# First bias by pieces, `past` ahead of the branch, and the first pair's q and k in units on two DMA queues

## The chip, the cores and the metric

The kernel runs on one core of one Trainium2 chip. A core has five engines that run side by side: TensorE (PE in the profile, with PEld for its weight loads), VectorE (DVE), ScalarE (ACT), GpSimd (POOL) and SyncE (SP), which in this kernel issues nearly all DMAs. Each engine takes its instructions in order; waits between engines are waits on semaphores. The metric is the device time of one execution in microseconds (us); lower is better.

## The reference, cut to what matters

One sample passes through three blocks: an attention with a band, a mask and an ALiBi bias, and two token and channel mixers. Only the start of the attention is touched here.

```python
B, H, S, D = 2, 8, 768, 64              # n_global = 8, n_local = 96
scores = scale * q @ k.T
rel = pos[:, None] - pos[None, :]
is_global = pos[None, :] < n_global
is_local = (rel >= 0) & (rel < n_local)
dist = where(is_global & ~is_local, n_local, abs(rel))
scores = where(is_global | is_local, scores - slopes[h] * dist, -1e9)
a = softmax(scores) ; attn = a @ v
x = attn as [B, S, H*D] ; x = moe(x) ; out = moe2(x)
```

## The kernel before

Attention runs in 24 **units**: two batches, four pairs of heads, and three units of two blocks of 128 queries in each pair. A unit u needs, for each of the pair's two heads, four score matmuls (L437) against the block's own 128 keys and the PREV = 96 keys before it with NG = 32 global ones, so 256 columns (128 for the first block of a sequence). VectorE adds the bias and takes the row's minimum of the negated score (L450), ScalarE takes the exponential (L574, L578), TensorE turns the result (L484), ScalarE or VectorE copies it out of PSUM (L496, L494), and TensorE multiplies with the values (L406). The loop of `attention_band` works on three units at once: scores of u, turning of u-1, values of u-2. Matmuls are recorded as several passes.

**Order.** Everything around the change is in a hand-written order (`manual_schedule`): each engine runs what is recorded for it, in the order of the code. Before the branch stand the loads of the first pair (`load_first`: two DMAs for k and two for q, of 2 and 4 blocks, all on SP), ten warming matmuls on zeros (L330), `constants`, `ramps` (three iotas on GpSimd, cast to float on ScalarE) and the first pair's values. Then every engine loads two words of `nv` into its registers (L913, first a pointer, then the value) and branches on them (L918): the band path for small n_global and n_local, a dense path otherwise.

**The bias.** Behind the branch `band_bias` makes one tile `base` of 128 x 384: `base0` (128 columns, for the first block of a sequence) and `base1` (256 columns: 96 `before`, 32 `seen`, 128 `own`). VectorE turns the counts to float (`nvf`, L290), makes `own` from `past` (a causal mask by affine select on GpSimd, L286), `before`, and the first NG columns of `base0` as the larger of `own` and `seen`; GpSimd makes `seen` (L292, L295); ScalarE copies the other 96 columns of `base0` (L308). Then each of the eight heads gets a scaled copy of all 384 columns: heads 0 and 1 on ScalarE (L317), heads 2 to 7 on GpSimd (L319).

**The loads of the next pairs.** Before the loop SP issues q and k of pair 1. In the loop, at the second unit of each pair, GpSimd sets ones in the next pair's value tiles (`tiles_v`, L360), and SP issues, in this order, that pair's v and twice a (`load_v`, L367, L369, L370), for pair 1 also a weight block (L125), and q and k of the pair after it (`load_qk`, L338, L339). In GpSimd's order the first of these `tiles_v` stands behind its six scaled copies of the bias; SP's v waits for it, and everything that SP issues later waits behind v. Numbering pairs 0 to 7, pair 1 begins with unit 3 and pair 2 with unit 6.

Of the kernel before, what the change touches and what calls it, by code (L numbers as in the profile page):

```python
# [15 lines left out]
F32 = mybir.dt.float32  # L16
# [3 lines left out]
AF = mybir.ActivationFunctionType  # L20
ALU = mybir.AluOpType
# [3 lines left out]
B, H, S, D = 2, 8, 768, 64  # L25
P = 128
NS = S // P
# [8 lines left out]
NG = 32  # L36
# [4 lines left out]
SCALE = 0.125  # L41
BIG = 2.56e11
# [14 lines left out]
def slope(h):  # L57
    return 2.0 ** (-(h + 1.0))
# [25 lines left out]
class Build:  # L84
# [139 lines left out]

    def constants(self, pool):
        nc = self.nc
        self.halfpi = pool.tile([P, 1], F32, name="halfpi")
        nc.vector.memset(self.halfpi, math.pi / 2)
        one = pool.tile([P, 1], F32, name="one")
        nc.scalar.activation(out=one, in_=self.halfpi, func=AF.Exp)  # L230
        self.ident = pool.tile([P, P], F32, name="ident")
        make_identity(nc, self.ident)

    def load_counts(self, pool):
        self.nvi = pool.tile([P, 4], I32, name="nvi")
        self.nvf = pool.tile([P, 4], F32, name="nvf")
        self.nc.sync.dma_start(out=self.nvi, in_=self.dram["nv"].broadcast_to([P, 4]))
# [24 lines left out]
    def ramps(self, pool):  # L262

        self.ramp = []
        for n, base, mult in ((P, 0, -1), (PREV, -PREV, -1), (NG, 0, 0)):
            ti = pool.tile([P, n], I32, name="ramp_i%d" % n)
            self.nc.gpsimd.iota(ti, pattern=[[1, n]], base=base, channel_multiplier=mult)
            tf = pool.tile([P, n], F32, name="ramp%d" % n)
            self.nc.scalar.copy(out=tf, in_=ti)
            self.ramp.append(tf)  # L270

    def band_bias(self, pool):

        nc = self.nc
        ng, nl = self.nvf[:, 0:1], self.nvf[:, 2:3]
        base = pool.tile([P, 3 * P], F32, name="base")  # L280
        base0, base1 = base[:, 0:P], base[:, P : 3 * P]
        before, seen, own = base1[:, 0:PREV], base1[:, PREV:P], base1[:, P : 2 * P]
        with self.tc.tile_pool(name="bb", bufs=1) as tp:
            d_own, d_prev, gcol = self.ramp
            past = tp.tile([P, P], F32, name="past")
            nc.gpsimd.affine_select(  # L286
                out=past, in_=d_own, pattern=[[-1, P]], compare_op=ALU.is_ge, fill=-BIG,
                base=0, channel_multiplier=1,
            )
            nc.vector.tensor_copy(out=self.nvf, in_=self.nvi)  # L290
            g = tp.tile([P, NG], F32, name="far_g")
            nc.gpsimd.tensor_scalar(  # L292
                out=g, in0=gcol, scalar1=ng, scalar2=-BIG, op0=ALU.is_ge, op1=ALU.mult
            )
            nc.gpsimd.tensor_scalar(out=seen, in0=g, scalar1=nl, scalar2=None, op0=ALU.subtract)  # L295
            nnl = tp.tile([P, 1], F32, name="nnl")
            nc.vector.tensor_scalar(out=nnl, in0=nl, scalar1=-1.0, scalar2=None, op0=ALU.mult)

            def near(out, t, dist, tag):

                far = tp.tile([P, t.shape[1]], F32, name="far" + tag)
                nc.vector.tensor_scalar(
                    out=far, in0=dist, scalar1=nnl, scalar2=-BIG, op0=ALU.is_le, op1=ALU.mult
                )
                nc.vector.tensor_tensor(out=out, in0=far, in1=t, op=ALU.add)

            near(own, past, d_own, "own")
            nc.scalar.copy(out=base0[:, NG:P], in_=own[:, NG:P])  # L308
            near(before, d_prev, d_prev, "prev")
            nc.vector.tensor_tensor(  # L310
                out=base0[:, 0:NG], in0=own[:, 0:NG], in1=seen, op=ALU.max
            )
        self.base = []
        for h in range(H):
            t = pool.tile([P, 3 * P], F32, name="base%d" % h)
            if h < 2:
                nc.scalar.activation(out=t, in_=base, func=AF.Copy, scale=slope(h) / SCALE)  # L317
            else:
                nc.gpsimd.tensor_scalar(  # L319
                    out=t, in0=base, scalar1=slope(h) / SCALE, scalar2=None, op0=ALU.mult  # L320
                )
            self.base.append((t[:, 0:P], t[:, P : 3 * P]))

# [16 lines left out]
    def load_first(self, pool):  # L342

        t = dict(
            q=pool.tile([P, S], F32, name="q_0_0", tag="q"),
            k=pool.tile([P, NS, KW], F32, name="k_0_0", tag="k"),
        )
        q, k = self.dram["q"][0, 0], self.dram["k"][0, 0]
        for i0, i1 in ((0, 2), (2, NS)):
            qs = slice(i0 * P, i1 * P)  # L350
            self.nc.sync.dma_start(out=t["k"][:, i0:i1], in_=k[:, i0:i1])
            self.nc.sync.dma_start(out=t["q"][:, qs], in_=q[:, qs])
        return t

# [512 lines left out]
    def run(self):  # L867
        nc, tc, dram = self.nc, self.tc, self.dram
        with ExitStack() as es:
            cp = es.enter_context(tc.tile_pool(name="const", bufs=1))  # L870
# [31 lines left out]
            with tc.tile_pool(name="pair0", bufs=1, side="right") as p0:  # L902
                with tc.manual_schedule():
                    self.load_counts(cp)
                    first = self.load_first(p0)
                    self.zero = self.x[1][:, 0, 0 : E // 2].bitcast(mybir.dt.bfloat16)
                    nc.vector.memset(self.zero, 0.0)
                    self.warm_up(WARM)
                    self.constants(cp)
                    self.ramps(p0)  # L910
                    self.tiles_v(p0, first, 0, 0)
                    self.load_v(first, 0, 0)
                    _, nv = nc.values_load_multi_w_load_instructions(dram["nv"])  # L913
                band = (
                    (nv[0] >= 0) * (nv[0] <= NG) * (nv[1] == 0)
                    * (nv[2] >= 1) * (nv[2] <= PREV + 1) * (nv[3] == 0)
                )
                with tc.If(band) as c:  # L918
                    with tc.tile_pool(name="bias", bufs=1, side="right") as bp, \
                            tc.tile_pool(name="pairs", bufs=2, side="right") as pp, \  # L920
                            tc.manual_schedule():
                        self.band_bias(bp)
                        self.attention_band(pp, first, h1)
                with c.Else():
                    self.counts(cp)
                    with tc.tile_pool(name="pairs", bufs=2, side="right") as pp:
                        self.attention_dense(pp, first, h1)
# [445 lines left out]
```

## Time and profile before

| | us |
|---|---|
| median of 3 runs (lowest, highest) | 492.79 (492.22, 492.97) |
| the profiled execution | 493.28 |
| its span in the trace | 491.5 |
| PE busy | 484.3 |
| DVE, ACT, POOL busy | 317.4, 262.9, 180.8 |

The granted TensorE clock is 1.00 over the whole span. In the trace all times count from the start of the span. A row of the timeline or of the chain gives start and duration; a row of waits gives the engine and line that waited, what ended the wait, the sum, the number and the longest; a row of a window gives, for each engine, busy time and number of instructions, then the granted clock, the busy share of the core's 16 DMA engines, and GB/s.

### The profile page before, as it was taken

What the parts mean: (1) busy time and instruction counts of PE and PEld (TensorE: products, weight loads), DVE (VectorE), ACT (ScalarE), POOL (GpSimd) and SP (SyncE); (2) the same over time, 40 slices, a digit from 0 to 9 for tenths busy, and PEclk for the clock granted to TensorE, in tenths of its full rate; (3) what the DMA queues carried; (4) which work ended last, traced back from release to release, by engine and by line L of the source; (5) the groups of instructions that cost most, each with busy time, mean ns of one, the idle gap of its engine ahead of it and who ended that gap; (6) DMA issues with size and microseconds to landing.
All of it is one profiled execution on the core that took longest, in us unless ns stands there. A gap on an engine that the chain in (4) does not pass through costs nothing.

```text
span 491.5 us, 7645 instructions
## 1 busy us (share of the span) xinstructions
PE 484.3 (99%) x2836; PEld 412.3 (84%) x2836; DVE 317.4 (65%) x671; ACT 262.9 (53%) x482; POOL 180.8 (37%) x187
## 2 busy tenths in 40 slices
PE   8999999999999999999999999999999999999997
PEld 4788888787888888888888888888888889988896
DVE  4688787854776689506656564687998866351442
ACT  6888777723565554204569464646776566322010
POOL 7345534430443575401323241334554633333000
PEclk9999999999999999999999999999999999999999
DMA  6687863401454545302444222524210101000012
GB/s 194 202 261 219 280 209 119 129 2 50 134 172 107 158 137 143 94 1 85 147 133 149 87 56 60 141 87 104 68 23 22 44 22 23 21 23 22 23 71 101
DMA packets 49022, 50.66 MB, mean 103 GB/s; under 512 B 20944, under 2 KB 39888, under 8 KB 48976
## 3 DMA queue, kind: packets, MB, share of 16 engines
q1 hardware_dynamic: 48976, 50.08, 34.6%
q8 instruction: 25, 0.41, 0.3%
q14 instruction: 21, 0.17, 0.1%
HBM read 42.21 MB, written 3.15 MB: 92 GB/s over the span
## 4 chain that ended last, share of the span: by engine, by line
PE 83%; DVE 5%; ACT 5%; POOL 3%; DMA 2%; issue 1%; DVEq 0%; SPq 0%; POOLq 0%; ACTq 0%
PE gp L96 20%; PE h L96 18%; PE y L96 13%; PE v L96 7%; PE mm L96 7%; PE o L406 5%; PE th L96 5%; PE t L484 4%; PE s L437 4%; DMA k<-k 2%; POOL base L319 1%; ACT cut_xt L789 1%; DVE x L1061 1%; DVE w L1154 1%; POOL s L1180 1%
## 5 line engine op out<-in xcount | busy, mean ns | idle before, releaser
L149 POOL TENSOR_TENSOR cvt<-cvt,cvs 128x512 int32<-128x512 int32 (+1 forms) x57 | 75.1, 1318 | 177.2 <-DVE cvt L148 144.0
L96 PE MATMUL h<-wc,g 128*128 128x512 f32 x432 | 101.7, 389 | 0.0
L96 PE MATMUL gp<-xh,wc 128*128 128x512 f32 (+1 forms) x384 | 97.1, 335 | 0.0
L96 PEld LDWEIGHTS h<-wc,g 128*128 128x128 f32 x432 | 79.6, 188 | 15.2
L96 PEld LDWEIGHTS gp<-xh,wc 128*128 128x128 f32 x384 | 67.2, 189 | 8.6 <-DVE g L708 0.2
L708 DVE SCALAR_TENSOR_TENSOR g<-gp,g 128x512 fp32r<-128x512 f32 (+1 forms) x48 | 26.7, 556 | 63.4 <-ACT g L706 63.1
L96 PE MATMUL gp<-xl,wc 128*128 128x512 f32 (+1 forms) x192 | 64.3, 335 | 0.0
L96 PE MATMUL y<-wri,s 128*128 128x256 f32 (+1 forms) x288 | 52.0, 335 | 0.2 <-POOL s L1180 0.2
L96 PE MATMUL y<-wri,z 128*128 128x256 f32 (+1 forms) x288 | 51.9, 335 | 0.0
L706 ACT ACTIVATE g<-gp 128x512 fp32r<-128x512 f32 (+1 forms) x48 | 23.4, 486 | 53.2 <-PE gp L96 53.2
L96 PEld LDWEIGHTS y<-wri,s 128*128 128x128 f32 x288 | 44.7, 189 | 6.4 <-POOL s L1180 0.4
L96 PEld LDWEIGHTS y<-wri,z 128*128 128x128 f32 x288 | 44.6, 188 | 5.9
L484 PE MATMUL t<-ident,e 128*128 128x128 f32 x176 | 48.1, 285 | 0.4 <-ACT at L496 0.4
L145 DVE SCALAR_TENSOR_TENSOR cvs<-cvt,cvs 128x512 int32<-128x512 int32 (+1 forms) x57 | 44.8, 787 | 0.1
L96 PEld LDWEIGHTS gp<-xl,wc 128*128 128x128 f32 x192 | 36.0, 188 | 4.7
L450 DVE CUSTOM_DVE_ANT_0 e<-s,base 128x256 f32<-128x256 f32 (+1 forms) x96 | 32.9, 397 | 9.1 <-PE s L437 7.1
L484 PEld LDWEIGHTS t<-ident,e 128*128 128x128 f32 x176 | 31.7, 184 | 8.1 <-issue 2.3
L139 ACT ACTIVATE cvt<-raw 128x512 f32<-128x512 f32 (+1 forms) x57 | 37.2, 653 | 2.2 <-issue 2.2
L140 ACT ACTIVATE cvs<-raw 128x512 int32<-128x512 uint16 (+1 forms) x57 | 37.4, 656 | 0.0
L96 PE MATMUL th<-s,xt 128*128 128x512 f32 x144 | 34.9, 391 | 0.0
L1157 ACT ACTIVATE w<-w 128x512 f32<-128x512 f32 x12 | 7.6, 632 | 49.4 <-DVE w L1154 49.4
L406 PE MATMUL o<-v,at 128*128 128x65 f32 x192 | 32.3, 252 | 0.0
(111 smaller groups left out, 839.9 us busy)
## 6 DMA issues: line engine op xcount, KB each, us to landing
raw<-w_ch SPq DMA_DIRECT2D x28, 512.0 KB, 4.1
raw<-w_tok SPq DMA_DIRECT2D x21, 512.0 KB, 4.2
k<-k SPq DMA_DIRECT2D x7, 480.0 KB, 5.6
v<-v SPq DMA_DIRECT2D x8, 384.0 KB, 3.7
out<-o SPq DMA_DIRECT2D x11, 256.0 KB, 2.0
q<-q SPq DMA_DIRECT2D x7, 384.0 KB, 4.7
raw<-w_theta SPq DMA_DIRECT2D x4, 512.0 KB, 4.0
a<-v SPq DMA_DIRECT2D x8, 240.0 KB, 4.5
```

Of the source, the lines that this page charges most:

```text
L96: self.nc.tensor.matmul(out, lhsT=a, rhs=b, start=first and i == 0, stop=last and i == n - 1)
L139: nc.scalar.activation(out=f(t), in_=f(top), func=AF.Copy, scale=2.0**-111)
L140: nc.scalar.activation(out=s, in_=nxt, func=AF.Copy, scale=2.0**-13)
L145: nc.vector.scalar_tensor_tensor(out=s, in0=t, scalar=-(1 << 31), in1=s, op0=ALU.bitwise_and, op1=ALU.bitwise_or)
L149: nc.gpsimd.tensor_tensor(out=t, in0=t, in1=s, op=ALU.add)
L406: self.nc.tensor.matmul(po[:, j * OW : j * OW + D + 1], lhsT=at, rhs=v[:, j * (D + 1) : (j + 1) * (D + 1)], start=first, stop=last,)
L437: nc.tensor.matmul(ps[j][:, ii, c0:], lhsT=t["q"][pj, i * P : (i + 1) * P], rhs=kf[pj, i * KW - P + c0 : i * KW + P], start=True, stop=True,)
L450: nc.vector.tensor_tensor_reduce(out=e, in0=ps[j][:, ii, c0:], in1=self.base[2 * hp + j][min(i, 1)], op0=ALU.add, op1=ALU.min, scale=-SCAL ...
L484: nc.tensor.transpose(pt[:, ii, c, :], e[j][:, ii, c * P : (c + 1) * P], self.ident)
L706: nc.scalar.activation(out=hi, in_=ps, func=AF.Relu if relu else AF.Copy)
L708: nc.vector.scalar_tensor_tensor(out=lo, in0=ps, scalar=0.0, in1=f(hi), op0=ALU.max, op1=ALU.subtract)
L1157: nc.scalar.activation(out=a, in_=t, func=AF.Abs)
```

## The change

- `constants` is split: a new `table`, called first, sets `halfpi` and starts ScalarE's table load; only `ident` stays in `constants`.
- `load_first` loads q and k in three pieces of two blocks each. q stays on SP. The first piece of k stays on SP, the other two are issued from ScalarE's queue, behind its table.
- `ramps` casts the iotas on VectorE and no longer on ScalarE, and makes `past` there, ahead of the branch, in a part of `x[1]` that is still free.
- In `band_bias` the larger-of of `own` and `seen` comes before `before`. Heads 0 and 1 get their bias in three pieces each: 96 columns from `own`, 32 from `base0`, 256 from `base1`. ScalarE's copy of 96 columns into `base0` stands behind these six. Heads 2 to 7 are as before on GpSimd, which reads all of `base`.

```diff
@@ constants @@
+    def table(self, pool):
+        self.halfpi = pool.tile([P, 1], F32, name="halfpi")
+        self.nc.vector.memset(self.halfpi, math.pi / 2)
+        one = pool.tile([P, 1], F32, name="one")
+        self.nc.scalar.activation(out=one, in_=self.halfpi, func=AF.Exp)
...
@@ ramps @@
-            self.nc.scalar.copy(out=tf, in_=ti)
+            self.nc.vector.tensor_copy(out=tf, in_=ti)
             self.ramp.append(tf)
+        self.past = self.x[1][:, 1, 0:P]
+        self.nc.gpsimd.affine_select(
+            out=self.past, in_=self.ramp[0], pattern=[[-1, P]], compare_op=ALU.is_ge, fill=-BIG,
+            base=0, channel_multiplier=1,
+        )
@@ band_bias @@
-            near(own, past, d_own, "own")
-            nc.scalar.copy(out=base0[:, NG:P], in_=own[:, NG:P])
-            near(before, d_prev, d_prev, "prev")
+            near(own, self.past, d_own, "own")
             nc.vector.tensor_tensor(
                 out=base0[:, 0:NG], in0=own[:, 0:NG], in1=seen, op=ALU.max
             )
...
+            near(before, d_prev, d_prev, "prev")
...
+        for h in range(2):
+            scaled(h, own[:, NG:P], NG, P)
+            scaled(h, base0[:, 0:NG], 0, NG)
+        for h in range(2):
+            scaled(h, base1, P, 3 * P)
+        nc.scalar.copy(out=base0[:, NG:P], in_=own[:, NG:P])
+        for h in range(2, H):
+            nc.gpsimd.tensor_scalar(
+                out=ts[h], in0=base, scalar1=slope(h) / SCALE, scalar2=None, op0=ALU.mult
+            )
...
@@ load_first @@
-        for i0, i1 in ((0, 2), (2, NS)):
-            qs = slice(i0 * P, i1 * P)
-            self.nc.sync.dma_start(out=t["k"][:, i0:i1], in_=k[:, i0:i1])
+        for i0 in range(0, NS, 2):
+            qs = slice(i0 * P, (i0 + 2) * P)
+            queue = self.nc.scalar if i0 else self.nc.sync
+            queue.dma_start(out=t["k"][:, i0 : i0 + 2], in_=k[:, i0 : i0 + 2])
             self.nc.sync.dma_start(out=t["q"][:, qs], in_=q[:, qs])
```

**VectorE ahead of the branch**, before (`x_66` is the tile of zeros for the warming matmuls, `ISA` begins the branch):

```order
L907 MEMSET x_66 128x256
L228 MEMSET halfpi 128x1
L913 TENSOR_LOAD nv_ptr
L913 TENSOR_LOAD nv
L918 ISA
```

and now:

```order
L232 MEMSET halfpi 128x1
L918 MEMSET x_66 128x256
L271 CAST ramp_132<-ramp_i_130 128x128 [waits Pool_49]
L271 CAST ramp_136<-ramp_i_134 128x96 [waits Pool_49]
L271 CAST ramp_140<-ramp_i_138 128x32 [waits Pool_49]
L924 TENSOR_LOAD nv_ptr
L924 TENSOR_LOAD nv
L929 ISA
```

Three casts that wait for GpSimd's iotas now stand ahead of VectorE's register loads.

**ScalarE behind the branch**, before (`base_303` and `base_305` are the bias of heads 0 and 1):

```order
L918 COMPARE_AND_BRANCH
L308 COPY base<-base 128x96 [waits DVE_49]
L317 ACTIVATE base_303<-base 128x384 [waits DVE_49,Activation_49]
L317 ACTIVATE base_305<-base 128x384
L574 ACTIVATE e_0_330<-e_0_330,mn_329 128x128 [waits DVE_49]
```

and now (heads 0 and 1 are `base_303` and `base_304`):

```order
L929 COMPARE_AND_BRANCH
L317 ACTIVATE base_303<-base 128x96 [waits DVE_49]
L317 ACTIVATE base_303<-base 128x32 [waits DVE_49]
L317 ACTIVATE base_304<-base 128x96
L317 ACTIVATE base_304<-base 128x32
L317 ACTIVATE base_303<-base 128x256 [waits DVE_49,Pool_49]
L317 ACTIVATE base_304<-base 128x256
L326 COPY base<-base 128x96
L584 ACTIVATE e_0_335<-e_0_335,mn_334 128x128 [waits DVE_49]
```

Two scaled copies became six, and the copy of 96 columns moved from ahead of them to behind them.

**GpSimd behind the branch**, before (`base_307` is head 2's bias):

```order
L918 COMPARE_AND_BRANCH
L286 AFFINE_SELECT past<-ramp_130 128x128 [waits Activation_49]
L292 TENSOR_SCALAR far_g<-ramp_138,nvf 128x32 [waits DVE_49,Activation_49]
L295 TENSOR_SCALAR base<-far_g,nvf 128x32 [waits Pool_49]
L319 TENSOR_SCALAR base_307<-base 128x384 [waits DVE_49,Activation_49]
```

and now (head 2 is `base_305`, head 3 `base_306`):

```order
L929 COMPARE_AND_BRANCH
L294 TENSOR_SCALAR far_g<-ramp_140,nvf 128x32 [waits DVE_49]
L297 TENSOR_SCALAR base<-far_g,nvf 128x32 [waits Pool_49]
L328 TENSOR_SCALAR base_305<-base 128x384 [waits DVE_49,Activation_49,Pool_49]
L328 TENSOR_SCALAR base_306<-base 128x384
```

`past` moved ahead of the branch. The first of the six scaled copies waits for VectorE and for ScalarE, as before; the ScalarE instruction that it waits for is the copy of 96 columns.

## Rows read from the trace of the kernel before

**Rows 1.** The page's part 1, TensorE: busy us, share of span, instructions.
```profile
PE 484.3 (99%) x2836; PEld 412.3 (84%) x2836; DVE 317.4 (65%) x671; ACT 262.9 (53%) x482; POOL 180.8 (37%) x187
```

**Rows 2.** Waits of PE, whole span: us in total, times, longest.
```profile
PE s L437 <- DMA q<-q: 0.8, 1, 0.8
PE s L437 <- DMA k<-k: 0.7, 1, 0.7
PE mm L96 <- ACT xh L706: 0.5, 1, 0.5
```

**Rows 3.** The chain that ended last, 0 to 25 us: start, us, what.
```profile
5.99 4.59 POOL base L319 x4
...
15.81 7.91 DMA k<-k
```

**Rows 4.** Timeline, 4 to 25 us, TensorE, GpSimd and SP's queue.
```profile
5.99 7.08 POOL L319 TENSOR_SCALAR base<-base 128x384 f32<-128x384 f32 x6 [0.39 <-DVE base L310]
13.27 0.38 SPq L367 DMA_DIRECT2D v<-v  x1
15.81 1.55 SPq L339 DMA_DIRECT2D k<-k  x1
23.86 0.93 PE L437 MATMUL s<-k,q 64*128 64x128 f32 x8 [0.70 <-DMA k<-k]
```

**Rows 5.** Line 913, the register loads by engine: ns min/median/max, first and last start.
```profile
L913 DVEq TENSOR_LOAD <-nv_ptr x1: 911/911/911, 0.8 to 0.8; - x1
L913 DVEq TENSOR_LOAD <-nv x1: 1346/1346/1346, 1.8 to 1.8; - x1
L913 ACTq TENSOR_LOAD <-nv_ptr x1: 1017/1017/1017, 2.0 to 2.0; - x1
L913 ACTq TENSOR_LOAD <-nv x1: 1051/1051/1051, 3.1 to 3.1; - x1
L913 SPq TENSOR_LOAD <-nv_ptr x1: 2880/2880/2880, 4.7 to 4.7; - x1
```

**Rows 6.** Timeline, 0 to 8 us: iotas, second k, and the bias.
```profile
1.26 0.50 POOL L267 IOTA ramp_i<- 128x128 int32 x3
2.12 0.43 SPq L351 DMA_DIRECT2D k<-k  x1
4.03 0.17 DVE L290 CAST nvf<-nvi 128x4 f32<-128x4 int32 x1 [2.89 <-DMA nvi<-nv]
4.56 0.50 POOL L292 TENSOR_SCALAR far_g<-ramp,nvf 128x32 f32<-128x32 f32 x1
5.15 0.45 POOL L295 TENSOR_SCALAR base<-far_g,nvf 128x32 f32<-128x32 f32 x1
5.28 0.27 ACT L308 COPY base<-base 128x96 f32<-128x96 f32 x1 [2.56 <-DVE base L305]
5.39 0.26 DVE L305 TENSOR_TENSOR base<-farprev,ramp 128x96 f32<-128x96 f32 x1
5.63 0.19 DVE L310 TENSOR_TENSOR base<-base 128x32 f32<-128x32 f32 x1
5.92 0.94 ACT L317 ACTIVATE base<-base 128x384 f32<-128x384 f32 x2 [0.37 <-DVE base L310]
```

**Rows 7.** Windows from v's issue to k's landing: busy, clock, DMA share, GB/s.
```profile
13.00:14.30 1.30, 1.16 (x12) 0.73 (x11) 0.71 (x3) 1.30 (x4) 0.63 (x4) 1.00 0.00 0
14.30:15.00 0.70, 0.70 (x9) 0.70 (x9) 0.66 (x5) 0.34 (x3) 0.65 (x1) 1.00 0.32 94
22.00:23.00 1.00, 1.00 (x12) 0.92 (x10) 1.00 (x5) 1.00 (x4) 0.26 (x3) 1.00 0.06 26
```

**Rows 8.** DMA queues, 15.7 to 15.8 and 16.9 to 17.0 us: packets, MB, share.
```profile
q8 instruction: 1, 0.02, 76.1%
...
q14 instruction: 1, 0.01, 35.9%
```

More of the change, by code (lines that the diff above doesn't have):

```diff
@@ L226, in constants @@
         nc = self.nc
[L227 to L230, printed above, removed]
         self.ident = pool.tile([P, P], F32, name="ident")
         make_identity(nc, self.ident)
+    def table(self, pool):
[3 more added lines that the diff above has]
+        self.nc.scalar.activation(out=one, in_=self.halfpi, func=AF.Exp)
     def load_counts(self, pool):
@@ L284, in band_bias @@
             d_own, d_prev, gcol = self.ramp
[L285 to L289, printed above, removed]
             nc.vector.tensor_copy(out=self.nvf, in_=self.nvi)
@@ L312, in band_bias, with scaled @@
             )
[L313 to L322, printed above, removed]
+            near(before, d_prev, d_prev, "prev")
+        ts = [pool.tile([P, 3 * P], F32, name="base%d" % h) for h in range(H)]
+        def scaled(h, src, c0, c1):
+            nc.scalar.activation(
+                out=ts[h][:, c0:c1], in_=src, func=AF.Copy, scale=slope(h) / SCALE
+            )
[8 more added lines that the diff above has]
+                out=ts[h], in0=base, scalar1=slope(h) / SCALE, scalar2=None, op0=ALU.mult
+            )
+        self.base = [(t[:, 0:P], t[:, P : 3 * P]) for t in ts]
     def warm_up(self, n):
@@ L904, in run @@
                     self.load_counts(cp)
+                    self.table(cp)
                     first = self.load_first(p0)
```

## The prediction

> **What bounds the kernel now.** I read three views in this order. The page's first part says that TensorE is busy for 484.3 of 491.5 us [rows 1], so the kernel is a nearly unbroken row of matmuls, and a change at the start counts only by what it does to the few breaks. The waits of TensorE name the breaks [rows 2]: 0.8 us for a q, 0.7 us for a k, then 0.5 us far behind the attention. The first is unit 1's, whose q comes in one large piece. The second is at 23.86, before the scores of unit 6, the first of pair 2 [rows 4]; the row says that it waited for pair 2's k. The third view, the chain that ended last, shows what that k hangs on [rows 3]: 4.59 us and more of GpSimd's scaled copies from 5.99 on, then a stretch of issues on SP, then 7.91 us for k itself. In code: GpSimd makes the bias of heads 2 to 7 in six copies from 5.99 for 7.08 us; only then it sets the ones in pair 1's value tiles; SP's v waits for that and is issued at 13.27; a, a, a weight block, q and k of pair 2 are issued behind it, k at 15.81 [rows 4], and k lands at 15.81 + 7.91 = 23.72 [rows 3]. The DMA engines had nothing to do from 13.0 to 14.3 [rows 7], so this block of loads starts when GpSimd lets it, not when the bandwidth does.
>
> So unit 6 starts at the later of two times: when TensorE is through with what stands ahead of it, 23.86 - 0.70 = 23.16, and when pair 2's k is there, 23.72. Behind unit 6 hardly anything can give time back, since the longest later wait is 0.5 us [rows 2] and comes from TensorE's own results. What unit 6 loses or gains goes to the end of the kernel.
>
> **What the change does to TensorE's side.** q and k of unit 1 come in pieces of two blocks; the wait of 0.8 us goes wholly or in part. It gives at most 0.8 us to units 1 to 5, and nothing to unit 6, which waits for k at 23.72 before and must now wait longer if k is later. By itself this edit is worth nothing: at the end it is hidden behind k.
>
> **What it does to the chain of GpSimd and k.** I go through it by steps.
>
> 1. VectorE's register loads. They began at 0.8 us and lasted 0.91 and 1.35 us [rows 5]. A load stands behind what its engine was given before; ScalarE's first load began at 2.0 us, behind its table. Now three casts stand ahead of VectorE's loads, and the last waits for the third iota, which ends at 1.26 + 0.50 = 1.76 [rows 6]. I take 1.84 for the start, an estimate, and for the lengths ScalarE's rows of about that time, 1.02 and 1.05 us [rows 5]: the loads end at 3.94 with 0.03 between them, where they ended at 3.11. Branch and `nvf` follow: `nvf` at 4.03 + 0.83 = 4.86 [rows 6].
> 2. The bias up to its last piece. `past` is ready now, but `seen` isn't: GpSimd starts it after `nvf` (4.86 + 0.17 + 0.04 = 5.07), its second step begins 0.59 us later (5.15 - 4.56) and takes 0.45: 6.11. The larger-of, 0.19 us, now stands ahead of `before` and waits for that: 6.33. `before` is two steps of 0.27 and 0.26 us, about 0.52 together: 6.85. In the kernel of before all was done at 5.63 + 0.19 = 5.82 [rows 6].
> 3. ScalarE. The four small pieces fit between 6.0 and 6.9 beside step 2. The two pieces of 256 columns start at 6.95; two of 384 took 0.94 us [rows 6], so I estimate 0.63 by columns: 7.58. Then comes the copy of 96 columns, 0.27 us [rows 6], which before ran at 5.28 beside VectorE: 7.83. GpSimd's first scaled copy reads these columns and starts some 0.16 us later (as 5.99 behind 5.82): **7.99 in place of 5.99, 2.0 us later**. ScalarE must be through its own branch by 6.3 for this. It has two issues now, by SP's row 0.43 us each [rows 6], so its loads begin at about 2.98 in place of 2.0 [rows 5] and it is through near 5.8.
> 4. The six copies last 7.08 us as before, so SP issues v at 15.27 in place of 13.27, and its first packet comes some 1.05 us later, since the engines stood still to 14.30 [rows 7]: 16.3.
> 5. How long the loads take. If they took what they took, k would land at 25.72. But from 22 to 23 us the share of the 16 DMA engines is 0.06 and they move 26 GB/s [rows 7]: that is one engine, alone, finishing its part of k, while fifteen were done about 1.8 us earlier. The only other traffic of that stretch is two packets of instructions, one begun between 15.7 and 15.8 that held its engine 76.1% of 16 x 0.1 = 1.22 us, one begun between 16.9 and 17.0, 35.9%, 0.57 us [rows 8]. Their sum, 1.79 us, is the delay of that engine. I conclude that both hit one engine and that k lands late by them. Instructions are fetched as the engines go on in the program, and around 16 us TensorE is about where it was. So the first fetch now falls largely ahead of v's first packet at 16.3 (at most 0.68 us of it are left, I take 0.4), and the second falls into the traffic as before. The delay shrinks from 1.79 to about 0.97, and 0.8 us of the 2.0 come back.
>
> Sum: k at 23.72 + 2.0 - 0.8 = 24.92, unit 6 later by **1.2 us**. Against its own time, the profiled execution of 493.28 us becomes 494.48; it lay 0.49 us above the median, so on the median: 492.79 + 1.2 = **494.0 us**.
>
> What else moves costs nothing: TensorE's warming matmuls start within 0.1 us of before (the zeros come second, behind a memset of one column), SP has as many DMAs ahead of the branch as before, and the casts that ScalarE loses were in a time when it waited 2.56 us [rows 6]. What no row shows is a DMA issued by ScalarE and what it does to the load behind it. The bounds are nothing (then ScalarE is through at about 4.9 and still waits for VectorE: no change to the sum) and SP's row, where a load behind eight DMAs took 2.88 us [rows 5]: then ScalarE is through near 7.5, its pieces end 1.1 us later, and GpSimd starts 3.1 us late. I take ScalarE's own row, since two DMAs are nearer to none than to eight, and keep the far end for the range.
>
> For step 5, the rows show fetches that cost a transfer 1.79 us. The Trainium skill, "Runtime: NRT & Kernel Launch", section "Instruction fetch mechanics", says that the sequencer streams instructions by its own DMA queue and that the cost of crossing a block is mostly hidden. By that rule the late engine has another cause, which would move along with the loads, and the full 2.0 us stay. No run here shows yet which holds; this is the second rival.
>
> **The rivals.**
> - *No change: both fetches fall ahead of v.* The place is pair 2's k. If the second fetch, too, ends before v's packets begin, or is tied to TensorE's progress and comes early, all 1.79 us come back: 23.72 + 2.0 - 1.79 = 23.93, unit 6 later by 0.2, 493.0 us. For it: the loads move by 2 us and the second fetch begins only 0.6 us behind the new first packet. Against it: nothing makes that fetch earlier. It decides from the point where more than 1.0 of the 2.0 us come back.
> - *The full shift.* The fetches don't matter, or hit again: 2.0 us, 494.8 us. For it: a fetch that is late by 0.6 us hits whole. Against it: 1.79 fits the late engine's delay.
> - *ScalarE's loads are held up* as SP's were: GpSimd 3.1 us late, TensorE's progress and its fetch about 1 us late as well, so some 1.0 of the delay comes back: about +2.1, at most 3.1: 494.9 to 495.9 us.
> - *VectorE isn't held up*, because its sequencer passes the waiting casts: the pieces on ScalarE start at about 5.8 by its own branch, GpSimd starts 1.2 us late at 7.2, v's packets at 15.5 meet both fetches, and little comes back: +0.8, 493.6 us. Against it: ScalarE's first load began only when its table was loaded [rows 5].
> - *Faster*: unit 6's k would have to land before 23.72. GpSimd cannot start before the copy of 96 columns, so only a faster transfer could do it; with all of 1.79 back this needs a shift below 1.8.
>
> **How the numbers follow.** Forecast +1.2 (from +0.9 to +1.7 as the first fetch overlaps): 0.43. Full shift 0.17. ScalarE held up 0.15. No change 0.12. VectorE not held up 0.09. Faster 0.04. A measurement of this kernel can tell some 0.2%, 1.0 us, from no change; so faster 0.04; same 0.12 + 0.09 and about a third of the forecast's own, 0.14: 0.35; slower 0.61. The range leaves out the ends: below 493.1 lies most of no change and faster, about 0.13, above 495.3 the late end of ScalarE held up, about 0.07. So 493.1 to 495.3, and 494.0 as the time.
>
> **What would show it.** In the profile of the changed kernel: VectorE's first register load near 1.84 and `nvf` near 4.9 (step 1); ScalarE's copy of 96 columns ending near 7.8 and GpSimd's first scaled copy at 8.0 (step 3); SP's v at 15.3 (step 4); between v's first packet and k's landing a tail of one engine of about 1 us, and the fetch of step 5 still near 15.8; unit 6's scores near 25.1 with a wait of about 1.9 us for k in place of 0.70. Wrong would be: a GpSimd that starts by 6.5, a k that lands before 23.9, or an end that keeps less than unit 6's shift, which would mean that TensorE had slack behind it that its waits do not show [rows 2]. A rest of 1.9 us on TensorE could also lower its clock; the two rests of before, 0.8 and 0.7, left the granted clock at 1.00.

## The result, and the profile after

The changed kernel takes **496.43 us** (median of 6 runs, 494.69 to 497.0), the kernel before 492.71 us in the same call: the ratio is 1.007, 95% interval 1.006 to 1.0081. It is slower by 3.7 us where 1.2 us were forecast, and lies above the range. The profiled execution took 496.39 us with a span of 494.6 us, 3.1 us more than the one of before [rows 1].

The page's first part and TensorE's waits in the changed kernel (total us, times, longest us):

```profile
PE 486.8 (98%) x2836; PEld 413.9 (84%) x2836; DVE 317.3 (64%) x674; ACT 262.8 (53%) x483; POOL 181.1 (37%) x187
```
```profile
PE s L447 <- DMA k<-k: 2.5, 1, 2.5
...
PE s L447 <- DMA q<-q: 0.3, 1, 0.3
...
PE mm L96 <- issue: 0.2, 1, 0.2
```

TensorE executes the same 2836 matmuls and is busy 2.5 us longer than in [rows 1]. That is the first sign of something that the forecast did not hold: a wait makes an engine idle, not busy. The waits of [rows 2] have moved as forecast in kind: unit 1 no longer waits 0.8 us for its q (the 0.3 us that is listed now is unit 0's), and the wait for pair 2's k grew from 0.7 to 2.5 us. The wait of 0.5 us far behind the attention is not in this trace.

The chain that ended last, in the same terms as [rows 3], has the same two links, both later:

```profile
8.81 4.59 POOL base L328 x4
...
18.63 7.21 DMA k<-k
```

The timeline of the first 9 us of the changed kernel (start, duration, engine, line, what; in brackets the idle time ahead and what ended it) shows how GpSimd came to 8.81:

```profile
0.73 1.28 ACT L234 ACT_TABLE_LOAD   x1 [0.73 <-PEq L1363]
0.91 0.87 ACTq L361 DMA_DIRECT2D k<-k  x2
1.53 0.63 DVE L271 CAST ramp<-ramp_i 128x128 f32<-128x128 int32 x3 [0.37 <-POOL ramp_i L269]
5.61 0.17 DVE L292 CAST nvf<-nvi 128x4 f32<-128x4 int32 x1 [3.45 <-issue]
6.50 0.48 POOL L297 TENSOR_SCALAR base<-far_g,nvf 128x32 f32<-128x32 f32 x1
6.84 1.66 ACT L317 ACTIVATE base<-base 128x96 f32<-128x96 f32 x6 [4.61 <-DVE base L307]
7.01 0.19 DVE L310 TENSOR_TENSOR base<-base 128x32 f32<-128x32 f32 x1 [0.28 <-POOL base L297]
7.42 0.26 DVE L307 TENSOR_TENSOR base<-farprev,ramp 128x96 f32<-128x96 f32 x1
8.40 0.25 ACT L326 COPY base<-base 128x96 f32<-128x96 f32 x1
```

Between the casts, which end near 1.84, and `nvf` at 5.61 stand VectorE's two register loads. Line 924 is the line of the loads now; the columns are those of [rows 5]:

```profile
L924 ACTq TENSOR_LOAD <-nv_ptr x1: 1536/1536/1536, 1.8 to 1.8; - x1
L924 DVEq TENSOR_LOAD <-nv_ptr x1: 1853/1853/1853, 1.9 to 1.9; - x1
...
L924 DVEq TENSOR_LOAD <-nv x1: 934/934/934, 3.8 to 3.8; - x1
L924 SPq TENSOR_LOAD <-nv_ptr x1: 2097/2097/2097, 5.3 to 5.3; - x1
```

The timeline of GpSimd, SP's queue and TensorE from 8 us on, against [rows 4]:

```profile
8.81 7.09 POOL L328 TENSOR_SCALAR base<-base 128x384 f32<-128x384 f32 x6 [1.82 <-DVE mn L460]
16.09 0.38 SPq L377 DMA_DIRECT2D v<-v  x1
16.57 0.50 SPq L379 DMA_DIRECT2D a<-v  x1
18.63 0.43 SPq L348 DMA_DIRECT2D k<-k  x1
25.98 0.99 PE L447 MATMUL s<-k,q 64*128 64x128 f32 x8 [2.47 <-DMA k<-k]
30.82 1.14 PE L447 MATMUL s<-k,q 64*128 64x256 f32 x8
```

GpSimd starts its six copies 2.82 us later (5.99 to 8.81), SP issues v 2.82 us later (13.27 to 16.09), k lands at 18.63 + 7.21 = 25.84 in place of 23.72, which is 2.12 us later, and unit 6 begins at 25.98 in place of 23.86, 2.12 us later. So 0.7 of the 2.82 us came back in the transfer. Unit 7 begins at 30.82. In the kernel of before, by its own timeline, it began here:

```profile
27.15 1.13 PE L437 MATMUL s<-k,q 64*128 64x256 f32 x8
```

That is 3.67 us earlier. Unit 6 thus took 4.84 us in place of 3.29, with the same matmuls and no wait in it. The windows of that stretch (its length; busy time and instructions of PE, PEld, DVE, ACT, POOL; granted clock of TensorE; DMA share; GB/s) say why:

```profile
26.50:27.00 0.50, 0.50 (x5) 0.10 (x3) 0.00 (x0) 0.00 (x0) 0.00 (x0) 0.72 0.90 216
27.00:30.00 3.00, 3.00 (x18) 3.00 (x19) 2.24 (x10) 1.68 (x5) 0.57 (x1) 0.50 0.98 283
30.00:30.50 0.50, 0.50 (x7) 0.50 (x6) 0.00 (x0) 0.41 (x2) 0.50 (x1) 0.87 1.01 402
```

TensorE rested 2.47 us ahead of unit 6, and between 26.5 and 27 us, when it was at work again, the granted clock fell to 0.50, the lower of its two levels (1.2 GHz), and came back between 30 and 30.5 us. That is 1.55 us of the loss in this execution, and it explains why TensorE is busy longer. Of the 3.67 us, 3.1 remain at the end of the span.

Instruction fetches, 15 to 17 us, against [rows 8] (share of 16 engines over 2 us, so 3.5% is 1.12 us of one engine and 1.1% is 0.35 us):

```profile
q8 instruction: 1, 0.02, 3.5%
q14 instruction: 1, 0.01, 1.1%
```

Both fetches now lie ahead of v's first packet, which comes near 17.1.

### The profile page after: what moved, and what is told of

Same layout as the page of the kernel before. It is cut to its first block, busy times and chain, and to the rows that moved or that the text cites. A ratio compares the mean times of both kernels' runs of the same rounds, so it can differ in the third digit from the quotient of the medians.

```text
span 494.6 us, 7652 instructions
## 1 busy us (share of the span) xinstructions
PE 486.8 (98%) x2836; PEld 413.9 (84%) x2836; DVE 317.3 (64%) x674; ACT 262.8 (53%) x483; POOL 181.1 (37%) x187
## 4 chain that ended last, share of the span: by engine, by line
PE 83%; DVE 5%; ACT 5%; POOL 3%; DMA 1%; issue 1%; DVEq 1%; SPq 0%; POOLq 0%; ACTq 0%
PE gp L96 20%; PE h L96 18%; PE y L96 13%; PE v L96 7%; PE mm L96 7%; PE o L416 6%; PE th L96 5%; PE t L494 4%; PE s L447 4%; DMA k<-k 1%; POOL base L328 1%; ACT cut_xt L799 1%; DVE x L1072 1%; DVE w L1165 1%; POOL s L1191 1%
## 5 line engine op out<-in xcount | busy, mean ns | idle before, releaser
L494 PE MATMUL t<-ident,e 128*128 128x128 f32 x176 | 49.2, 290 | 0.4 <-ACT at L506 0.4
```

What stands on the lines that cost most here:

```text
L494: nc.tensor.transpose(pt[:, ii, c, :], e[j][:, ii, c * P : (c + 1) * P], self.ident)
```

## The experiments

The theory after the result: the front delays GpSimd by 2.82 us, GpSimd delays v and k, the rest that TensorE then has ahead of unit 6 is long enough for its clock to fall, and both together are the loss. The rivals: the loss comes from units 0 to 5, whose q and k now land later or otherwise; or k's transfer, not GpSimd, is what became slower; or the clock's fall is hidden by waits behind it. Three kernels make one part of the change alone, two take a suspected step of the front away, two add work on GpSimd to the kernel before, three free v from GpSimd, and two fill TensorE's rest.

### The parts alone

**Bias by pieces, alone** (the kernel before, with the larger-of ahead of `before`, the pieces on ScalarE and the copy of 96 columns behind them):

```diff
+        for h in range(2):
+            scaled(h, own[:, NG:P], NG, P)
+            scaled(h, base0[:, 0:NG], 0, NG)
+        for h in range(2):
+            scaled(h, base1, P, 3 * P)
+        nc.scalar.copy(out=base0[:, NG:P], in_=own[:, NG:P])
...
```

> The kernel before with the bias of heads 0 and 1 by pieces and the copy of 96 columns behind them; casts, past and loads as before. Chain theory: GpSimd starts near 7.4 in place of 5.99, k lands 1.0 to 1.5 us later, the end is 493.7 to 494.3 us. If the late register loads are the whole loss: nvf stays at 4.0, the time at 492.8 us or below.

Measured: 494.26 us, ratio 1.0044 (1.0019 to 1.0068). `nvf` stays at 4.05, GpSimd starts at 7.30 (+1.31), v is issued at 14.59, and unit 6 waits 2.01 us and begins at 25.27.

**q and k by units, k on ScalarE's queue behind `table`, alone:**

```diff
-        for i0, i1 in ((0, 2), (2, NS)):
-            qs = slice(i0 * P, i1 * P)
-            self.nc.sync.dma_start(out=t["k"][:, i0:i1], in_=k[:, i0:i1])
+        for i0 in range(0, NS, 2):
+            qs = slice(i0 * P, (i0 + 2) * P)
+            queue = self.nc.scalar if i0 else self.nc.sync
+            queue.dma_start(out=t["k"][:, i0 : i0 + 2], in_=k[:, i0 : i0 + 2])
...
+                    self.table(cp)
```

> The kernel before with q and k by units and k's later pieces on ScalarE's queue; casts on ScalarE and bias as before. Contention theory: the register loads lengthen by 0.3 to 0.9 us and GpSimd starts 0.2 to 0.8 us late; unit 1 no longer waits 0.8 us for q, which does not reach unit 6; the end is 492.9 to 493.6 us. Without contention: unit 6 as before, 492.8 us.

Measured: 493.36 us, ratio 1.0013 (0.9997 to 1.0029). GpSimd starts at 6.71 (+0.72), and unit 6 at 24.08 (+0.22). The prediction gave this part no effect on VectorE or GpSimd. What it does there stands in the register loads of VectorE (line 917 here), whose casts are not ahead of them in this kernel:

```profile
L917 DVEq TENSOR_LOAD <-nv_ptr x1: 919/919/919, 0.8 to 0.8; - x1
...
L917 DVEq TENSOR_LOAD <-nv x1: 2060/2060/2060, 1.8 to 1.8; - x1
```

The second load starts when it did in [rows 5] and lasts 0.71 us longer (2.06 for 1.35 us).

**Casts on VectorE and `past` ahead, alone:**

```diff
-            self.nc.scalar.copy(out=tf, in_=ti)
+            self.nc.vector.tensor_copy(out=tf, in_=ti)
             self.ramp.append(tf)
+        self.past = self.x[1][:, 1, 0:P]
+        self.nc.gpsimd.affine_select(
...
```

> The kernel before with the casts on VectorE and past ahead of the branch; loads and bias as before. If the casts hold VectorE's register loads: they start at 1.85 in place of 0.82, nvf moves from 4.03 to about 4.85, GpSimd starts 0.6 to 0.9 us late, the end is 493.2 to 493.7 us. If not: 492.8 us or below.

Measured: 494.15 us, ratio 1.0033 (1.0015 to 1.0051). VectorE's loads start at 1.87, where the forecast had 1.84, they take 1.20 and 1.05 us, and `nvf` comes at 5.07; GpSimd starts at 6.96 (+0.97). So each of the three parts delays GpSimd by itself: 1.31 + 0.72 + 0.97 = 3.00 us, against 2.82 together, and none of them makes the kernel faster. In the profiled execution the wait was 1.79 us, and the clock fell (same columns as the windows above):

```profile
25.00:26.00 1.00, 1.00 (x11) 0.67 (x8) 0.24 (x3) 0.00 (x0) 0.07 (x1) 0.82 1.22 238
26.00:28.00 2.00, 2.00 (x13) 2.00 (x13) 1.97 (x10) 1.07 (x3) 0.00 (x0) 0.50 1.11 221
```

### Two suspected steps in the front

**The changed kernel with the copy of 96 columns ahead of the six pieces:**

```diff
+        nc.scalar.copy(out=base0[:, NG:P], in_=own[:, NG:P])
         for h in range(2):
...
             scaled(h, base1, P, 3 * P)
-        nc.scalar.copy(out=base0[:, NG:P], in_=own[:, NG:P])
```

> The changed kernel with ScalarE's copy of 96 columns back ahead of the six pieces of the bias. Chain theory (the time is lost where GpSimd's scaled copies start later, so that pair 2's k lands later and unit 6 waits): GpSimd starts behind VectorE's last step, near 7.85 in place of 8.81, k and unit 6 come 0.6 to 1.0 us earlier (unit 6 at 25.0 to 25.4), TensorE's rest shrinks from 2.5 to below 1.9 us, and the end is 494 to 495.5 us in place of 496.4. Front theory (the loss is in units 0 to 2, by the late bias itself): ScalarE's pieces start 0.15 us later, so the same time or 0.2 us more.

Measured: 496.04 us, ratio 1.0059 (1.0042 to 1.0076). GpSimd starts 0.98 us earlier than in the changed kernel (7.83), v is issued 0.97 us earlier (15.12), but k lands only 0.4 us earlier, and unit 6 begins at 25.61. Step 3 of the prediction is right about the copy; it is worth 1 us on GpSimd. The end hardly shows it: the transfer keeps most of it, and in the profiled execution the clock falls here too, after a rest of 1.53 us.

**The changed kernel with all of the first pair's k on SP's queue:**

```diff
-            queue = self.nc.scalar if i0 else self.nc.sync
+            queue = self.nc.sync
```

> The changed kernel with all three pieces of k issued by SP. Contention theory (the two DMAs of ScalarE, which start at 0.9 us, lengthen the first loads and the register loads, 1.85 us for VectorE's first): VectorE's register loads fall back to about 1.0 us each, nvf moves from 5.6 to about 4.9, GpSimd starts near 8.1 in place of 8.8, and the end is 494.5 to 495.8 us. If the casts ahead of VectorE's loads are the whole delay: nvf stays at 5.6 and the time at 496.4 us.

Measured: 494.93 us, ratio 1.0044 (1.0026 to 1.0061). The register loads of VectorE and GpSimd's copies:

```profile
L924 DVEq TENSOR_LOAD <-nv_ptr x1: 1216/1216/1216, 1.9 to 1.9; - x1
...
L924 DVEq TENSOR_LOAD <-nv x1: 598/598/598, 3.1 to 3.1; - x1
```
```profile
7.84 7.08 POOL L328 TENSOR_SCALAR base<-base 128x384 f32<-128x384 f32 x6 [1.83 <-DVE mn L460]
```

The two loads take 1.81 us in place of 2.79, `nvf` comes at 4.64 in place of 5.61, and GpSimd starts at 7.84, close to the 7.99 that the prediction had. So the two DMAs, issued early on ScalarE's queue and not later on SP's, cost GpSimd 0.97 us. By the tile `nvi`, whose transfer SP issues at 0.74 in all these kernels, other transfers feel them as well: it takes 2.8 us from issue to landing in the kernel before and in this one, and 3.3 us in the changed kernel and in the one with the units alone.

### The cost of the delay itself

**The kernel before with one, or two, extra copies of head 2's bias on GpSimd ahead of the six**, and nothing of the change (the cut shows two; with one it is `range(1 ...)`):

```diff
+                for _ in range(2 if h == 2 else 0):
+                    nc.gpsimd.tensor_scalar(
+                        out=t, in0=base, scalar1=slope(h) / SCALE, scalar2=None, op0=ALU.mult
+                    )
```

> The kernel before with one extra copy of head 2's scaled bias on GpSimd ahead of the six: nothing else of the front is touched. Theory (whatever makes GpSimd's copies late makes v, k and unit 6 late): v 1.17 us later, near 14.4, k 0.7 to 1.2 us later, unit 6 at 24.5 to 25.1, end 493.5 to 494.3 us. Rival (the change loses its time elsewhere in the front, and k has slack): end 492.5 to 492.9 us. By the fetches' account of the prediction, k is later by less than v, by up to 0.8 us.

> The kernel before with two extra copies of head 2's scaled bias on GpSimd. Theory: v 2.34 us later, near 15.6, k 1.6 to 2.4 us later, unit 6 at 25.4 to 26.2, with a rest of TensorE of over 2 us ahead of it, a granted clock of 0.50 behind it in most runs and an end of 495.5 to 496.5 us; without that fall 494.5 to 495.0 us. Rival as with one copy: 492.5 to 492.9 us. If the rest alone brings the clock's fall, this kernel shows it with none of the change's edits in it.

Measured: with one 493.94 us, ratio 1.0032 (1.0017 to 1.0046); with two 496.02 us, ratio 1.0071 (1.0054 to 1.0088), as much as the changed kernel, whose ratio is 1.007. GpSimd's delay alone, made by other means, makes the kernel that much slower, so the rival that all of it is lost in units 0 to 5 falls. That the two sizes agree so closely is partly chance, though: in the profiled execution with two copies unit 6 begins 0.95 us earlier than in the changed kernel and the clock stays up (494.57 us), while the other three runs carry a fall of the clock.

The two timelines, SP's queue and TensorE's unit 6, with one copy:

```profile
14.59 0.38 SPq L371 DMA_DIRECT2D v<-v  x1
15.07 1.42 SPq L373 DMA_DIRECT2D a<-v  x1
18.45 0.43 SPq L343 DMA_DIRECT2D k<-k  x1
24.96 0.93 PE L441 MATMUL s<-k,q 64*128 64x128 f32 x8 [1.64 <-DMA k<-k]
```

and with two:

```profile
15.75 0.38 SPq L371 DMA_DIRECT2D v<-v  x1
16.24 0.68 SPq L373 DMA_DIRECT2D a<-v  x1
18.48 0.43 SPq L343 DMA_DIRECT2D k<-k  x1
25.03 0.93 PE L441 MATMUL s<-k,q 64*128 64x128 f32 x8 [1.68 <-DMA k<-k]
```

v is 1.16 us apart, k's issue 0.03 us and unit 6 0.07 us. With one copy an instruction fetch runs from 15.06 to 16.07, and SP's issue at 15.07 lasts 1.42 us in place of 0.48 to 0.50, and the weight block's, beside a second and smaller fetch, 0.82 in place of 0.43; with two copies the larger fetch is nearly over by the time SP comes to that issue. So a fetch seems to delay the loads by holding up an issue that runs beside it. In the traces of all 14 kernels (before, after and the twelve here), 14 of the 15 issues of SP between 8 and 20 us that last over 0.6 us overlap a fetch, and eight of the nine that overlap the larger one end 0.38 to 0.43 us behind its end. In the kernel before it was k's own issue, with 1.55 us [rows 4]. But an overlap is not enough: 13 other issues overlap a fetch and last 0.38 to 0.53 us, v's own, the first of the block, in all seven kernels where it does. The fifteenth (1.62 us, at 11.35 in the next section's first kernel) has no fetch beside it, and what held it is open.

The expectation that the clock would fall in most runs with two copies came true in 3 of 4: these have a mean granted clock of 0.995 to 0.997 and spans of 494.2 to 494.5 us; the fourth, the profiled one, has 0.999 and 492.8 us. The fall is worth 1.4 us there, between executions of one and the same kernel.

### Pair 1's value tiles set early

SP's v waits for GpSimd because the ones in the value tiles of pair 1 are set behind the six copies. Two kernels set these tiles ahead of the bias: the changed kernel, and the kernel before with the same edit.

```diff
-            pairs[order[1]] = self.load_qk(pairs_pool, *order[1], bufs=2)
+            pairs[order[1]] = dict(self.load_qk(pairs_pool, *order[1], bufs=2), **self.ahead)
...
-                    self.tiles_v(pairs_pool, pairs[nx], *nx)
+                    if oi > 0:
+                        self.tiles_v(pairs_pool, pairs[nx], *nx)
...
+                        self.ahead = {}
+                        self.tiles_v(pp, self.ahead, 0, 1)
                         self.band_bias(bp)
```

> The changed kernel with the ones of pair 1's value tiles set by GpSimd ahead of the bias, so that SP's v, a, a, weights, q and k of pairs 1 and 2 no longer wait for the six scaled copies. Chain theory: v is issued near 9.7, k lands near 20, unit 6 starts when TensorE comes to it, near 23.5, the clock stays, and the end is 492.0 to 492.7 us, the whole loss gone. Front theory: the loss of units 0 to 2 stays, 495 us or more.

> The kernel before with the ones of pair 1's value tiles set ahead of the bias. Chain theory: pair 2's k no longer holds unit 6, TensorE comes to it at 23.16 in place of 23.86, and the end is 0.5 to 0.8 us earlier, about 492.1 us. If something else is as late (the weights' scaling, a later pair's k): no change, 492.8 us.

Measured: the changed kernel with it 492.84 us, ratio 0.9998 (0.9988 to 1.0008), the kernel before with it **492.09 us, ratio 0.9983 (0.9973 to 0.9992)**. In the changed kernel GpSimd still starts its copies at 8.77, yet v is issued at 10.33 and unit 6 begins at 23.64 without a wait:

```profile
8.77 7.08 POOL L328 TENSOR_SCALAR base<-base 128x384 f32<-128x384 f32 x6 [1.83 <-DVE mn L460]
10.33 0.38 SPq L377 DMA_DIRECT2D v<-v  x1
23.64 0.93 PE L447 MATMUL s<-k,q 64*128 64x128 f32 x8
```

So nearly all of the front's delay reaches the end by GpSimd, value tiles, v, k. A little takes another road: with the same edit the kernel before has its unit 6 at 23.35, 0.29 us earlier, and unit 5, too, is 0.29 us earlier there (20.20 against 20.49). That kernel:

```profile
9.48 0.38 SPq L367 DMA_DIRECT2D v<-v  x1
...
23.35 0.93 PE L437 MATMUL s<-k,q 64*128 64x128 f32 x8
```

It gains the 0.5 us that unit 6 lost to k (23.86 to 23.35), and beats both kernels. With every delay of k gone, 0.8 us are to be had by the medians; 0.5 of them are seen at unit 6.

**The changed kernel with early value tiles and all of k on SP's queue:**

```diff
-            queue = self.nc.scalar if i0 else self.nc.sync
+            queue = self.nc.sync
...
```

> The changed kernel with pair 1's value tiles set ahead of the bias, and all pieces of the first pair's k on SP's queue. Theory (GpSimd's delay reaches the end only through v, which waits for pair 1's value tiles, so with that taken away nothing of the front matters but units 0 and 1): GpSimd's first scaled copy at 7.8 us in place of 8.8, v issued near 9.5, k there by 22 us, unit 6 without a wait at 23.2 to 23.6, end 492.0 to 492.6 us. Rival (the pieces of k on SP cost unit 0 and 1 as much as GpSimd gains): unit 6 at 23.6 or later, end 492.8 us or more.

Measured: 492.45 us, ratio 1.0001 (0.9991 to 1.001); unit 6 at 23.43. That is within what the theory expected, but no better than with k on ScalarE (0.9998), and the intervals do not part the two.

### The clock's fall

**The changed kernel with 11 warming matmuls ahead of unit 6**, which keep TensorE at work while it waits for k:

```diff
+                    if u == 6:
+                        self.warm_up(FILL6)
                     exps = scores(u)
```

> The changed kernel with 11 warming matmuls on zeros ahead of unit 6's scores, about 2.4 us of work in the place of TensorE's rest of 2.5 us. Clock theory (a part of the loss is the clock, granted at 0.50 from about 26.7 to 30.1 us): unit 6 starts at 25.9 to 26.2 as before, the clock stays at 1.00, and the end comes 1.0 to 1.5 us earlier, 495 to 495.5 us. If the rest alone is the loss: the same 496.4 us.

Measured: 496.77 us, ratio 1.0081 (1.0064 to 1.0098). The clock stays at 1.00, unit 6 begins at 26.34, and by the transposes near 100 us TensorE is 1.2 us ahead of the changed kernel. But the gain is gone at the end. The waits of TensorE have a new one, which no other kernel of this study shows at this size; it stands near 120 us:

```profile
PE mm L97 <- issue: 1.1, 1, 1.1
```

An instruction fetch ends 0.07 us before TensorE goes on (121.70 and 121.77 us). Whether that is the cause isn't known: the next kernel has a fetch at the same place (121.53 to 121.95) without such a wait. Two readings were left: the extra instructions shift the place of all that follow, and the wait comes from there; or TensorE has a fixed time to make there, whatever happens ahead.

**The same with 12 warming matmuls, and six value matmuls left out of the dense path**, which does not run on these inputs, so that the instructions behind stand about where they stood:

```diff
+FILL6 = 12
+SKIP = ((0, 0, 0, 0), (0, 0, 1, 0))
...
+                                if (b, hp, i, j) in SKIP and 0 < k < 4:
+                                    continue
```

> The changed kernel with 12 warming matmuls ahead of unit 6, as in the run with 11, and with six value matmuls left out of the dense path, which doesn't run on these inputs, so that TensorE's instructions behind the attention stand about where they stand in the changed kernel. Expected in every case: unit 6 at 26.0 to 26.4 us, granted clock 1.00 at 27 to 30 us. Theory (the clock's fall costs some 1.2 to 1.5 us that go to the end, and the new wait of 1.14 us behind the attention in the run with 11 matmuls came from the place of the instructions): that wait is gone, end 495.0 to 495.5 us. Rival (TensorE has a fixed amount to wait there whenever it comes early, so that the clock's fall is hidden): a wait of about 1 us again near 120 us, end 496.2 to 496.8 us.

Measured: 495.28 us, ratio 1.0063 (1.0039 to 1.0087). Timeline of TensorE and window:

```profile
23.50 2.75 PE L341 MATMUL warm<-x 128*128 128x512 bf16 x12
26.18 0.93 PE L449 MATMUL s<-k,q 64*128 64x128 f32 x8
...
29.48 0.92 PE L449 MATMUL s<-k,q 64*128 64x256 f32 x6
```
```profile
27.00:30.00 3.00, 3.00 (x30) 2.86 (x30) 2.59 (x13) 2.38 (x6) 0.37 (x1) 1.00 0.99 306
```

The wait of 1.1 us is gone, and where the changed kernel got through 18 matmuls from 27 to 30 us this one gets through 30. Unit 7 begins at 29.48, 1.34 us earlier than in the changed kernel, although unit 6 begins 0.2 us later, and the span ends 1.1 us earlier (493.5 against 494.6 us). So in this pair of traces the clock's fall does reach the end, and the rival that waits behind it hide it falls. The medians point the same way (495.28 against 496.43 us), but the intervals of the two ratios overlap. That the place of the instructions makes the wait of 1.1 us is borne out by this one kernel; what it is about the place isn't known.

How often the clock falls: each run lists its mean granted clock; only profiled executions show where it fell. In the seven kernels whose profile shows TensorE resting 1.5 to 2.5 us ahead of unit 6, 23 of 53 runs have a mean of 0.992 to 0.997; the other 30 have 0.999 or 1.0. With a rest of 0.57 us (the units alone) it is 1 of 10 runs, with 0.70 us (the kernel before) none of 60, without a wait at unit 6 none of 30, with the rest filled none of 9. Within one kernel the runs with a low mean are longer by 1.4 us (two extra copies; 1.45 in the changed kernel, 493.3 to 494.75 us between the medians of the spans) to 3.0 us (bias by pieces). A fall like that of the changed kernel's trace does not explain 3.0 us; four runs have a mean of only 0.992 or 0.993, an estimated 7 to 8 us at the lower level (0.008 of 495 us, twice) against about 3.4 us in that trace, and no trace shows such a run. Nor does the length of the rest decide alone: in the profiled executions the clock fell after rests of 2.47, 1.79 and 1.53 us, and stayed at 1.00 after 2.01, 1.68, 1.68 and 1.64 us. What decides is open.

## Why the prediction was wrong

The place, the direction and the road were right: pair 2's k, behind GpSimd's six copies, sets the start of unit 6, and most of what unit 6 loses goes to the end. The size was wrong by 2.5 us, and two steps of the prediction failed: the lengths of VectorE's register loads in step 1, and the clock, which the sum left at nothing.

- **Step 1 (VectorE's register loads): start right, lengths mis-sized.** The loads begin at 1.87, forecast 1.84. The forecast took 1.02 and 1.05 us for their lengths, from ScalarE's rows of the kernel before; they take 1.85 and 0.93. `nvf` comes at 5.61 in place of 4.86, 0.75 us late. The cause shown: with k's pieces on SP's queue they take 1.22 and 0.60, so ScalarE's two DMAs cost 0.97 us; with the casts alone, and no DMA on ScalarE's queue, they take 1.20 and 1.05 us, near the forecast. The prediction bounded "what it does to the load behind it" for ScalarE's own loads alone, and did not ask what those DMAs do to the other engines' loads. Behind this stands a wrong picture of "behind its table": ScalarE issues its DMAs at 0.91, while the table is still being loaded (0.73 to 2.01), not at 2.0, so that they run beside the count's transfer and the register loads. That the loads lengthen because these share the way to memory is argued; the runs show only that they lengthen when those DMAs are issued there.
- **Step 2** was 0.08 us short (2.07 us from `nvf` to the last piece of the bias, forecast 1.99). **Step 3** was right: from there to the end of the copy of 96 columns 0.97 us, forecast 0.98 (its 7.58 and 0.27 make 7.85, not 7.83), and 0.16 us on to GpSimd. ScalarE's loads end at 4.7, well ahead of its first piece at 6.84, so the rival that they are held up did not happen. GpSimd's 8.81 in place of 7.99 is step 1's 0.75 and step 2's 0.08 us.
- **Step 4** was right: SP issues v 2.82 us later, exactly GpSimd's delay.
- **Step 5 (the fetches give 0.8 us back): size right by luck, mechanism only in part.** v's issue to k's landing takes 9.75 us, 10.45 before, so 0.7 us come back. But by the prediction's own account all of 1.79 us should have, since both fetches now end ahead of v's first packet: the condition of its rival "no change" came about, without that rival's price. The prediction tied the fetches to TensorE's place; they began 0.6 and 0.7 us earlier (15.17 and 16.23), while TensorE was 0.36 us later at unit 5. What sets their place isn't known. The late engine has indeed gone: the last of k's 128 packets ends 0.41 us behind the 120th, 1.70 before. What the prediction missed is the issue on SP that a fetch can stretch; and the transfer up to the 120th packet of k now takes 0.6 us more. Over the kernels that wait for k at unit 6, this time runs from 9.14 us (two extra copies) to 10.55 (bias by pieces), and the fetches do not account for all of that. That part is open.

  The Trainium skill, "Runtime: NRT & Kernel Launch", section "Instruction fetch mechanics", says that the cost of crossing a block of instructions is mostly hidden. What a fetch costs the engine that fetches no run here shows; beside a fetch SP's issues are not always spared: 1.42 us for one of 0.48 to 0.50.
- **Not in the sum: the clock.** The prediction's last sentence named it and gave it no price, because two rests of 0.7 and 0.8 us had left the clock at 1.00. The forecast's own rest of 1.9 us lay outside what those two rows could tell, so a fall belonged among the rivals, with a bound from a row of TensorE at the lower level. It cost 1.55 us in the profiled execution, and 4 of 6 runs have it.

With these, the sum in the profiled execution: GpSimd +2.82, back in the transfer -0.70, unit 6 +2.12; the clock +1.55; 3.67 us at unit 7, of which 0.57 came back further on. The wait of 0.5 us behind the attention [rows 2], which this trace lacks, may be a good part of it; that TensorE misses it by being late isn't shown, since with the copy of 96 columns ahead it comes nearly as late (unit 7 at 30.47) and has a wait of 0.6 us there. That leaves 3.1 us of span. The prediction let hardly anything come back behind unit 6; this was a small error on the other side.

The edit on q did not help units 1 to 5 either. Unit 1's wait of 0.8 us is gone, but unit 0 begins at 5.94 in place of 4.93, with a wait for its q, and unit 5 at 20.29 in place of 19.93.

## What to carry to other kernels

A DMA that is put on another engine's queue starts when that queue lets it, which may be earlier than the engine's compute row suggests; ask what small transfers and loads of every engine run at that moment, not only what stands behind it on its own queue. When a forecast makes a rest of a TensorE that is otherwise busy longer than any rest in the trace, put a price on its clock, from a row at the lower level, and give that case a chance of its own. And where a wait hangs on a step that has nothing to do with it (here ones in a value tile behind six copies), move that step: this alone made the kernel before 0.17% faster, which none of the three parts of the change did.

## What the runs showed of the hardware that was not expected

- ScalarE's DMA issues ran at 0.91 and 1.33 us while its table load ran from 0.73 to 2.01: the queue did not wait for the table.
- A load of one count into a register took from 0.51 us to 2.88 us [rows 5] in these kernels. It was longer where two more transfers had been issued just ahead: 1.85 against 1.22 us, and 2.06 against 1.35.
- An issue of a DMA on SP that overlaps an instruction fetch can take up to 1.73 us, most others take 0.35 to 0.5 us; 14 that overlap one were stretched, 13 were not (casts alone):

```profile
14.24 0.38 SPq L367 DMA_DIRECT2D v<-v  x1
14.73 1.73 SPq L369 DMA_DIRECT2D a<-v  x1
16.51 0.49 SPq L370 DMA_DIRECT2D a<-v  x1
```

- After a rest of 1.5 to 2.5 us in an otherwise unbroken row of matmuls, TensorE's granted clock fell to 0.50 in three of seven profiled executions (2.47, 1.79 and 1.53 us; not after 2.01, 1.68, 1.68 and 1.64), and the mean clock of these kernels' runs is low in 23 of 53. In the three the clock was 1.00 through the rest; the fall came with matmuls at work again (26.5 to 27 us in the changed kernel, unit 6 at 25.98).
